# A two-layer transformer kernel whose planner takes its settings from a string: another string, read twice as often

## The chip, the cores and the metric

The kernel runs on one core of a Trainium2 chip. The metric is the device time of one execution in microseconds (us). A core has TensorE (PE, matmuls; PEld is its weight load), VectorE (DVE), ScalarE (ACT), GpSimd (POOL) and SyncE (SP, which issues the DMA transfers). Each engine works through its own list of instructions in order, and they wait for each other by semaphores.

## The reference

Two equal rounds of a 32-head attention block and a feed-forward block on 2048 tokens of width 512, with normalisation in front of each and residual additions. Input setup and casts are left out.

```python
def _A_ref(x, wqkv, wo):
    B, S, D = x.shape
    H = 32; Dh = D // H
    qkv = (lambda x, *d: x.transpose(*d))((x @ wqkv).reshape(B, S, 3, H, Dh), 2, 0, 3, 1, 4)
    q, k, v = qkv[0], qkv[1], qkv[2]
    scale = Dh ** -0.5
    scores = jnp.einsum("bhqd,bhkd->bhqk", q, k) * scale
    p = _softmax(scores, axis=-1)
    o = jnp.einsum("bhqk,bhkd->bhqd", p, v)
    return (lambda x, *d: x.transpose(*d))(o, 0, 2, 1, 3).reshape(B, S, D) @ wo

def _B_ref(x, w1, b1, w2, b2):
    y = _layernorm(x, axis=-1)
    h = _gelu(jnp.einsum("bsd,df->bsf", y, w1) + b1)
    return jnp.einsum("bsf,fd->bsd", h, w2) + b2

x = A_x
x = x + _A_ref(_layernorm(x, axis=-1), A_wqkv, A_wo)
x = x + _B_ref(_layernorm(x, axis=-1), B_w1, B_b1, B_w2, B_b2)
x = x + _A_ref(_layernorm(x, axis=-1), A_wqkv, A_wo)
x = x + _B_ref(_layernorm(x, axis=-1), B_w1, B_b1, B_w2, B_b2)
```

## The kernel before

**A program that plans itself.** The Python code does not write out its instructions in a fixed order. Every piece of work is a task for one engine, with the resources it reads and writes, a priority and an assumed duration. A scheduler (class `Sched`) simulates the five engines with these durations, always takes the task that can start first, and among the ready tasks of an engine the one of the smallest priority number. The result is one fixed list of instructions for each engine. What the chip runs is these lists, with semaphore waits between them; nothing is decided at run time.

**The work.** The two attention layers are called 1 and 3. The scores of a layer are cut into tiles of 128 keys by 512 queries (in layer 3's last units, 256 queries) for one head: 4096 tiles in all. Four heads make a head group; a segment is a head group's work for one unit of queries. For a tile:

- Line 1470, `score`: TensorE writes a score tile to one bank of PSUM, the accumulation memory. It uses one quarter of the array's rows, so up to four such matmuls run side by side.
- Line 1455: ScalarE takes the exponential of a group of tiles at once. Groups alternate between three banks and two, and a group is called an exponential group here. There are 1273 of them. In the opening part of layer 1, the first 64 groups, each has two.
- Lines 1555 and 1588: some tiles go to VectorE instead. Line 1555 approximates the exponential by shifting the score into the bits of a 16-bit float, and line 1588 makes three further shifted copies of two tiles at once, which are averaged by the value matmuls.
- Line 1658: value matmuls, which multiply the exponentials by the values and accumulate in bank 6. They use a quarter of the array's columns, so four run side by side. Line 1650 adds a correction row at the start of some segments.
- Line 1688 and after it: at the end of a segment VectorE transposes the accumulator, and the result is normalised.

Beside this run the linear parts: line 950 (queries, keys and values), 1737 (attention output), 1792 (first linear of the feed-forward block), 1835 (second linear). Line 1827 is the GELU on ScalarE, in which no exponential can run. Lines 927 and 1784 are transposing DMA transfers that bring normalised tokens in front of lines 950 and 1792.

**The bound over all keys.** Softmax needs an upper bound of each row's scores. It comes from the norms of all keys known so far: line 1157 takes the maximum, line 1159 transposes it on TensorE, line 1160 reduces, line 1162 takes a root on POOL, line 1163 builds a small matrix, line 1165 is a small matmul, line 1166 gives the scale, line 1196 makes the query tile. Layer 1 begins with the first 4 key blocks (part 0), layer 3 with the first 12. When all 16 are there, the bound is taken anew for part 1, and no score of part 1 can begin before.

**Fillers.** After planning, `refill` walks through TensorE's list and puts in matmuls on zeros (lines 1359, 1361, 1363; full array, row quarter, column quarter) where the plan has a gap on TensorE, as wide as the gap, as long as TensorE's planned use over the last 3.414 us is under 55%.

**The settings.** Class `Hint` holds six numbers that the planner reads, ten sets of them (`MODES`) and a string `ORDER`, in which a digit names a set. `flow_scores` counts the exponential groups with `gi` and reads the next digit after every `STEP` groups:

```python
if gi % Hint.STEP == 0:
    HINT.at(gi // Hint.STEP)
```

`D_IDLE` is how little work VectorE must have in front of it for a further tile to go there. `PV_LEAST` is how full a batch of value matmuls has to be. `HOLD_LATE` lengthens the time for which other matmuls are held back in front of scores that are due. `PV_NEAR` is how soon exponentials must be ready to be counted for a batch. `LIN2` caps the priority number of the later halves of linear work: 9 leaves it as it is, 0.9 puts these halves ahead of value matmuls, which have 1.0. `D_STEAL` lets VectorE take the last tile of a group of three where it has no work.

Of the kernel before, what the change touches and what calls it, by code (L numbers as in the profile page):

```python
# [507 lines left out]
class Hint:  # L508
    BASE = dict(D_IDLE=1.2, PV_LEAST=0.75, HOLD_LATE=0.4, PV_NEAR=0.7, LIN2=9, D_STEAL=0)
    MODES = (dict(), dict(D_IDLE=0.8), dict(D_IDLE=1.7), dict(PV_LEAST=0.6), dict(PV_LEAST=0.9), dict(HOLD_LATE=0.2), dict(HOLD_LATE=0.6), dict(PV_NEAR=0.4), dict(LIN2=0.9), dict(D_STEAL=1.0))  # L510
    STEP = 8
    ORDER = '0355550015621021500127723542380000551183094330404202738042440023535555121020004212005090903453421320027044075009578104471100282939255971103200420580357499912000'

    def mode(self, k):
        self.__dict__.update(self.BASE)
# [2 lines left out]
    def at(self, step):  # L518
        self.mode(int(self.ORDER[step], 36) if step < len(self.ORDER) else 0)

# [5 lines left out]
class Builder:  # L526
# [844 lines left out]
    def flow_scores(self):  # L1371
# [14 lines left out]
        while True:  # L1386
            if gi % Hint.STEP == 0:
                HINT.at(gi // Hint.STEP)
            self.advance()
# [629 lines left out]
```

## Time and profile before

| | |
|---|---|
| time, median of 3 runs | 1563.72 us (1562.58 to 1564.21) |
| span of the profiled execution | 1564.7 us |
| instructions | 39699 |
| ScalarE: exponentials, line 1455 | 1433.7 us busy, 1273 groups |
| VectorE: lines 1555 and 1588 | 638.1 and 559.9 us busy |
| TensorE: scores, line 1470 | 599.1 us busy |
| TensorE: value matmuls, line 1658 | 3525 on ScalarE's exponentials, 1083 and 3249 on VectorE's |
| TensorE: fillers | 487 of line 1359, 465 of line 1361, 1808 of line 1363 |
| granted TensorE clock, mean | 0.999 |

A group's row names the line, engine, operation and tiles, then the count, the busy time and the mean duration of one, and behind the second bar the idle time of the engine just before them and what ended it. Matmuls overlap, so their summed durations exceed the time they take. In rows in order of time, the first number is the start, the second the length, and a number in brackets the idle time before it with its releaser.

### The profile page before, as it was taken

How to read it: one execution, taken by the hardware profiler on the slowest of the kernel's cores; microseconds unless marked ns; L12 is line 12 of the kernel's file. 1: busy time of each engine (PE TensorE's matmuls, PEld its weight loads, DVE VectorE, ACT ScalarE, POOL GpSimd, SP SyncE). 2: the span in 40 equal slices, each digit the busy share in tenths (PEclk: the TensorE clock that was granted, in tenths of full speed). 3: DMA queues.
4: the chain of work that ended last, by engine and by line, in shares of the span. 5: the costliest groups of instructions: out<-in, count | busy, mean ns of one | idle time of the engine just before them, and what ended most of it. 6: DMA issues, size and time to landing. Idle time of an engine off the chain costs nothing.

```text
span 1564.7 us, 39699 instructions
## 1 busy us (share of the span) xinstructions
PE 1517.7 (97%) x16674; PEld 483.1 (31%) x16674; DVE 1459.9 (93%) x3256; ACT 1517.1 (97%) x1361; POOL 321.2 (21%) x558
## 2 busy tenths in 40 slices
PE   9999999999999999999999999999999999999998
PEld 3222222232223222222222322222232232344444
DVE  7699999999999899989999799999899999999894
ACT  8979999999999999999999999999999999999996
POOL 3575312001210021203222227410001000020100
PEclk9999999999999999999999999999999999999999
DMA  7663111203311232223832232310102000211110
GB/s 162 116 143 97 35 31 32 61 17 85 85 40 46 47 76 59 61 48 92 145 45 66 56 82 63 62 25 22 35 16 44 22 17 25 41 45 32 43 30 19
DMA packets 212451, 88.69 MB, mean 57 GB/s; under 512 B 183307, under 2 KB 207152, under 8 KB 212272
## 3 DMA queue, kind: packets, MB, share of 16 engines
q1 hardware_dynamic: 212272, 86.16, 24.9%
q8 instruction: 130, 2.13, 0.6%
q14 instruction: 49, 0.40, 0.1%
HBM read 34.65 MB, written 19.48 MB: 35 GB/s over the span
## 4 chain that ended last, share of the span: by engine, by line
ACT 34%; DVE 33%; PE 29%; issue 2%; POOL 1%; SPq 1%; DMA 1%; POOLq 0%; DVEq 0%
ACT PT L1455 33%; DVE dp L1555 13%; DVE dp L1588 10%; PE ps L1470 9%; PE ps L1658 8%; PE ps L1835 3%; PE ps L1792 2%; PE ps L950 2%; DVE accT L1688 2%; DVE n L1015 1%; ACT h L1827 1%; PE ps L1359 1%; DVE sq L991 1%; DVE h L1816 1%; PE ps L1068 1%
## 5 line engine op out<-in xcount | busy, mean ns | idle before, releaser
L1455 ACT ACTIVATE PT<-ps 128x1536 bf16<-128x1536 f32 (+1 forms) x1273 | 1433.7, 1285 | 28.5 <-PE ps L1470 25.1
L1555 DVE TENSOR_SCALAR dp<-ps 128x512 uint16<-128x512 f32 x960 | 638.1, 679 | 36.7 <-PE ps L1470 34.2
L1470 PE MATMUL ps<-QT,KT 32*128 32x512 bf16 (+1 forms) x4608 | 599.1, 359 | 19.6 <-ACT PT L1455 6.8
L1588 DVE TENSOR_SCALAR dp<-dp 128x1024 uint16<-128x1024 uint16 (+1 forms) x1452 | 559.9, 427 | 4.6 <-PE ps L1658 1.6
L1658 PE MATMUL ps<-PT,V 128*17 128x512 bf16 (+1 forms) x3525 | 483.8, 358 | 0.2 <-ACT PT L1455 0.2
L1658 PE MATMUL ps<-dp,vs 128*17 128x512 bf16 (+1 forms) x3249 | 467.6, 357 | 0.9 <-DVE dp L1588 0.4
L1470 PEld LDWEIGHTS ps<-QT,KT 32*128 32x128 bf16 x4608 | 161.1, 91 | 545.9 <-ACT PT L1455 286.3
L1196 POOL TENSOR_SCALAR QT<-qraw,scl,qbias 128x512 bf16<-128x512 bf16 (+1 forms) x83 | 72.3, 872 | 764.6 <-PE ps L1470 758.1
L1658 PE MATMUL ps<-dp,V 128*17 128x512 bf16 (+1 forms) x1083 | 227.1, 358 | 1.6 <-DVE accT L1688 0.6
L1363 PE MATMUL ps<-zw 128*32 128x448 bf16 (+23 forms) x1808 | 172.2, 321 | 0.8 <-DVE dp L1555 0.7
L1658 PEld LDWEIGHTS ps<-dp,vs 128*17 128x17 bf16 x3249 | 119.1, 88 | 115.4 <-issue 87.2
L1658 PEld LDWEIGHTS ps<-PT,V 128*17 128x17 bf16 x3525 | 116.9, 88 | 92.8 <-issue 78.5
L1361 PE MATMUL ps<-zw 32*128 32x444 bf16 (+5 forms) x465 | 132.8, 317 | 0.0
L1359 PE MATMUL ps<-zw 128*128 128x448 bf16 (+17 forms) x487 | 114.7, 334 | 3.2 <-DVE onec L754 2.1
L1792 PE MATMUL ps<-yT,wf 128*128 128x512 bf16 (+3 forms) x396 | 101.7, 361 | 3.1 <-DVE dp L1588 1.3
L950 PE MATMUL ps<-wqkv,xnT 128*128 128x512 bf16 x336 | 93.4, 382 | 5.8 <-DVE dp L963 2.2
L1363 PEld LDWEIGHTS ps<-zw 128*32 128x32 bf16 x1808 | 62.5, 95 | 27.8 <-DVE dp L1555 4.6
L1658 PEld LDWEIGHTS ps<-dp,V 128*17 128x17 bf16 x1083 | 55.5, 88 | 41.4 <-issue 24.1
L1221 POOL TENSOR_SCALAR vs<-V 128x340 bf16<-128x340 bf16 (+2 forms) x72 | 61.8, 859 | 26.1 <-PE ps L1658 15.1
L1688 DVE STREAM_TRANSPOSE accT<-ps 128x512 f32<-128x512 f32 (+1 forms) x88 | 57.8, 657 | 7.1 <-PE ps L1658 7.0
L1816 DVE TENSOR_SCALAR h<-ps,b1c 128x512 bf16<-128x512 f32 (+2 forms) x88 | 61.9, 703 | 1.9 <-PE ps L1792 1.5
L1359 PEld LDWEIGHTS ps<-zw 128*128 128x128 bf16 x487 | 37.6, 98 | 64.7 <-issue 40.0
(182 smaller groups left out, 885.5 us busy)
## 6 DMA issues: line engine op xcount, KB each, us to landing
vs<-vs_scr SPq DMA_DIRECT2D x56, 255.0 KB, 2.7
wf<-in_B_w_dram SPq DMA_DIRECT2D x90, 128.0 KB, 2.9
q_scr<-qk SPq DMA_DIRECT2D x20, 256.0 KB, 2.1
k_scr<-qk SPq DMA_DIRECT2D x12, 256.0 KB, 2.0
out_dram<-xres SPq DMA_DIRECT2D x16, 128.0 KB, 1.8
vs_scr<-vs SPq DMA_DIRECT2D x8, 255.0 KB, 2.9
xres<-in_A_x_dram SPq DMA_DIRECT2D x7, 256.0 KB, 3.2
v_scr<-vst SPq DMA_DIRECT2D x12, 136.0 KB, 1.7
```

The lines of the kernel that those rows point to most:

```text
L950: yield Task("pe", prio if c0 == 0 else min(prio, HINT.LIN2), [I(lambda e, c=c: e.matmul(self.ps[:, b, :], lhsT=xnT[:, c, :], rhs=self.wqk ...
L1359: fn = lambda e: e.matmul(self.ps[:, b, 0:w], lhsT=self.zw[:, 0:128], rhs=self.zw[:, 0:w], start=st, stop=st, skip_group_check=True)
L1361: fn = lambda e: e.matmul(self.ps[:, b, 0:w], lhsT=self.zw[32 * p:32 * p + 32, 0:128], rhs=self.zw[32 * p:32 * p + 32, 0:w], start=st, sto ...
L1363: fn = lambda e: e.matmul(self.ps[32 * p:32 * p + 32, b, 0:w], lhsT=self.zw[:, 0:32], rhs=self.zw[:, 0:w], start=st, stop=st, skip_group_c ...
L1455: S_.submit(Task("act", 1e-5 * gi, [I(lambda e, pt=pt, n=n, b0=b0: e.activation(out=self.PT[:, pt:pt + n, :], in_=self.ps[:, b0:b0 + n, :] ...
L1470: return [I(lambda e, kb=kb, i=i: e.matmul(self.ps[:, b, i * W:(i + 1) * W], lhsT=self.KT[32 * hp:32 * hp + 32, hg, kb * 128:(kb + 1) * 12 ...
L1555: self.S_.submit(Task("dve", 0.0, [I(lambda e: e.tensor_scalar(out=self.dp[:, u, w * 512:(w + 1) * 512], in0=self.ps[:, b, :], scalar1=BIT ...
L1588: yield Task("dve", pr, [I(lambda e, k=k, v=v: e.tensor_scalar(out=self.dp[:, v, 0:N], in0=self.dp[:, u, 0:N], scalar1=float(SHIFT[k]), sc ...
L1658: ops.append((nth[j, sh] + 0.1 * i, I(lambda e, hp=hp, v=v, ap=ap[:, i * W:(i + 1) * W], first=first and i == 0, W=W: e.matmul(self.ps[32 ...
L1688: yield Task("dve", 0.3, [I(lambda e: e.transpose(self.accT[:, a, 0:W], self.ps[:, ACCB, 0:W]), [("ps", ACCB)], [RA], 0.17 + 0.535 * W / 5 ...
L1792: yield Task("pe", pr if c0 == 0 else min(pr, HINT.LIN2), [I(lambda e, c=c: e.matmul(self.ps[0:M, b, off:off + W], lhsT=self.w1(fc, c), rh ...
L1816: S_.submit(Task("dve", pr - 0.7, [I(lambda e, fc=fc, M=M, b=b: e.tensor_scalar(out=hv[0:M, fc * W:(fc + 1) * W], in0=self.ps[0:M, b, 0:W] ...
```

## The change

The string is another one, of 319 digits instead of 160, and a digit holds for four exponential groups instead of eight. The sets of settings are the same. No other line differs (but for an empty line at the end of the file).

```diff
 class Hint:
     BASE = dict(D_IDLE=1.2, PV_LEAST=0.75, HOLD_LATE=0.4, PV_NEAR=0.7, LIN2=9, D_STEAL=0)
     MODES = (dict(), dict(D_IDLE=0.8), dict(D_IDLE=1.7), dict(PV_LEAST=0.6), dict(PV_LEAST=0.9), dict(HOLD_LATE=0.2), dict(HOLD_LATE=0.6), dict(PV_NEAR=0.4), dict(LIN2=0.9), dict(D_STEAL=1.0))
-    STEP = 8
-    ORDER = '0355550015621021500127723542380000551183094330404202738042440023535555121020004212005090903453421320027044075009578104471100282939255971103200420580357499912000'
+    STEP = 4
+    ORDER = '1000505400844554053031008034310130004043277211200001031009349005902383344374250110710071520000700010897013450230200545450055021090000330009921105703053220050405100500340302221091514024010003201130050000322000100000400300044000720830007030033701430000245354444034510580430030403022240093200204095050982000792049091440853'
```

The new string was found by following many partial orders of the work at once. How the two programs differ instruction by instruction is part of the working below.

## The prediction

> **What bounds the kernel now.** I read the page's busy shares first, then the groups by line, then the waits of ScalarE, then busy time by stage, then ScalarE and TensorE in order of time around the largest waits.
>
> ```profile
> PE 1517.7 (97%) x16674; PEld 483.1 (31%) x16674; DVE 1459.9 (93%) x3256; ACT 1517.1 (97%) x1361; POOL 321.2 (21%) x558
> ...
> L1455 ACT ACTIVATE PT<-ps 128x1536 bf16<-128x1536 f32 (+1 forms) x1273 | 1433.7, 1285 | 28.5 <-PE ps L1470 25.1
> ```
>
> PE's 97% holds zero matmuls (lines 1359, 1361, 1363) that only fill gaps, so it isn't the bound by itself. ACT has no filler: it idles 47.6 us of the span of 1564.7, and 25.1 of them stand before an exponential whose scores were not there. So the bound is the chain scores, exponential, with TensorE's order deciding how seldom ACT starves. ACT's busy time is a floor, its idle time is what an order can win. By stage (columns: window, length, then busy us of PE, PEld, DVE, ACT, POOL, clock, DMA share, GB/s):
>
> ```profile
> 0.00:80.00 80.00, 74.71 (x502) 24.27 (x503) 58.78 (x147) 73.29 (x86) 34.67 (x85) 1.00 0.68 139
> 80.00:140.00 60.00, 56.20 (x534) 16.74 (x533) 56.49 (x124) 50.95 (x48) 42.14 (x76) 1.00 0.62 136
> 140.00:800.00 660.00, 646.52 (x6594) 189.96 (x6590) 642.02 (x1409) 652.36 (x571) 123.06 (x201) 1.00 0.26 59
> 800.00:1000.00 200.00, 191.86 (x1973) 57.26 (x1965) 184.93 (x408) 194.51 (x176) 76.56 (x132) 1.00 0.30 66
> 1000.00:1540.00 540.00, 528.62 (x6934) 184.35 (x6926) 511.76 (x1159) 535.45 (x468) 43.29 (x60) 1.00 0.14 31
> 1540.00:1564.70 24.70, 19.82 (x159) 10.49 (x158) 5.88 (x13) 10.59 (x17) 1.48 (x4) 1.00 0.07 17
> ```
>
> ACT's idle by these stages is 6.7, 9.1, 7.6, 5.5, 4.5 and 14.1 us. The first 20 us and the last 24 hold fixed chains; some 26 us can be fought for. Three places hold half of that:
>
> ```profile
> 81.29 2.96 ACT L1455 ACTIVATE PT<-ps 128x1024 bf16<-128x1024 f32 x3 [0.21 <-PE ps L1470]
> 90.59 4.77 ACT L1455 ACTIVATE PT<-ps 128x1536 bf16<-128x1536 f32 x4 [6.35 <-PE ps L1470]
> ...
> 696.92 3.28 ACT L1455 ACTIVATE PT<-ps 128x1024 bf16<-128x1024 f32 x3 [2.43 <-PE ps L1470]
> ...
> 1215.70 1.45 ACT L1455 ACTIVATE PT<-ps 128x1536 bf16<-128x1536 f32 x1 [1.78 <-PE ps L1470]
> ```
>
> At 90.59 the next scores need the bound over all keys of layer 1 (lines 1157 to 1166). At 696.92 TensorE ran five matmuls of the second linear and 22 value matmuls between two scores. At 1215.70 it stood before line 1792, whose last transposed input was issued on SP at 1209.9 and let it begin at 1213.44 (the tile's landings take 2.5 to 4.2 us).
>
> **What the change does, step by step.** No line of code that issues work differs; other settings reorder it. So the cost lies in the order of the two programs' instructions, compared engine by engine. Counts: SP 524 and POOL 562 instructions in both, so no transfer is added. On ACT, 590 exponentials of three banks become 586 and 683 of two become 687. On DVE line 1555 goes from 960 to 964 tiles, and line 1588 gains 12 half-width rows (24 to 36). The fillers fall from 2760 to 2550.
>
> (a) ACT's work: by form a three-bank exponential takes 1515 ns and a two-bank one 1086, so 4 x 0.429 = -1.7 us. Between 0 (it comes back as waiting) and -1.7; I take -1.7, since ACT is the floor.
>
> (b) DVE's four tiles: 4 x 0.60 (two of line 1555 take 1.20 in the chain) plus 12 x 0.27 (the shortest of line 1588) = 5.6 us on an engine that idles 105 us. Cost 0, hidden by that idle time; up to +5.6 if all of it falls where DVE is full. Nearer to 0, since the tiles per eight heads differ by at most 4.
>
> (c) The first bound over keys. Rows before and after it:
>
> ```profile
> 82.79 0.39 PE L1470 MATMUL ps<-QT,KT 32*128 32x512 bf16 x2
> ...
> 87.02 0.23 PE L1159 MATMUL ps<-ident,nm 128*32 128x128 bf16 x1
> ...
> 89.94 0.82 PE L1470 MATMUL ps<-QT,KT 32*128 32x512 bf16 x7
> ```
>
> From 83.11, when line 950 follows the last score, to 89.94 are 6.83 us, of which 2.92 are the bound's own chain from line 1159 on. ACT's wait is that gap less the exponential still running (1.13, to 84.24) plus 0.65 from first score to exponential: 6.35. Before line 1159 the old program has six matmuls of line 950, eight of 1658 and fillers of 36 x 448 and 4 x 267 columns in four tiles side by side, 1.79 us. The new one has four of line 1650, eight of 1658 and 1341 columns (0.56 us). At 0.0606 us a value matmul (16 in 0.97 in the chain) that is 0.73 + 0.56 = 1.29, so the gap is 1.3 + 2.9 = 4.2, and the gain -2.6. Between 0 (the keys come no sooner) and -3.6 (the last two score groups now stand together, one exponential of 1.0 more to run meanwhile). I take -2.6, the rows' own difference.
>
> (d) A new bare stretch: at the second bound over keys of layer 3 the old program keeps scores between line 1159 and line 1165, the new one keeps none. Its 7 value matmuls (0.42) and 0.36 us of filler before line 1159, plus 2.92, make a gap of 3.7. Two exponentials (30 take 33.69 in the chain, so 2.25) can be queued: 3.7 - 2.25 + 0.65 = +2.1. Bounds 0 (a third is queued) and +3.2 (only 1.13 is).
>
> (e) The burst at 694 us is gone: outside the stretches behind a GELU, which hide under the 5 to 8 us that ACT spends on it, no score-free stretch over 1.5 us is left between the two bounds but (d). -2.4; 0 if another takes its place.
>
> (f) All other waits: 25.1 less 6.96 around 90.59, 2.43 and the 2.73 around 1215 leaves 13.0. Priced by rows (0.238 us a full matmul, five in 1.19 in the chain), score-free stretches exceed 1 us by 32.1 us in all in the old order and 26.1 in the new, 19% less: -2.5. Bounds 0 and -9.8: fillers on TensorE's own time fall from 147.3 to 135.8 us (columns at 0.417 ns; eight of 448 took 1.60), 1.7 of it in (c), and the rest would be all span.
>
> (g) Tail: 1344 columns of filler instead of 322 wait for the last head: +0.4 (0 to +0.9). The rest of the tail's order is the same.
>
> (h) Queues: transposes and loads on SP shift by a few places past each other. The nearest price is the stall at 1215: 1.78 + 0.56 + 0.39 = 2.73 us. I take 0, one such landing as before; -2.7 to +2.7 for none or two.
>
> Sum: -1.7 - 2.6 + 2.1 - 2.4 - 2.5 + 0.4 = -6.7. The profiled span of 1564.7 lies 1.0 over the median of 1563.72; 1558.0 of span is 1557.0 us.
>
> [...]
>
> ```profile
> 1212.00:1213.00 1.00, 0.10 (x2) 0.00 (x0) 1.00 (x4) 1.00 (x2) 0.00 (x0) 1.00 0.00 0
> ...
> 1214.00:1215.00 1.00, 1.00 (x7) 0.17 (x5) 0.00 (x0) 0.00 (x0) 0.00 (x0) 0.50 0.00 0
> ```
>
> The granted clock fell to 0.5 for 3.4 us after TensorE stood empty for only 1.34 us. [...]
>
> **The rivals.** Slower: late landings. TensorE is in order, so a matmul placed too early for its transposed input holds back the scores behind it, and the clock falls too. For it: 1215.70, and a new order sets all such places anew. Against it: the old order has one such stall in 1564 us. At 2.73 each, four more (6.7 + 3.1 over 2.73 is 3.6) decide: 1557.0 + 10.9 = 1567.9.
>
> No change: the waits move. If (d) costs the full 6.35 of the first bound (+4.2) and a burst like (e) stands elsewhere (+2.4), it ends at 1563.6. For it: (d) is plainly new. Against it: two groups can be queued there.
>
> More: all of the filler's fall is span, (f) at -9.8: 1549.7. For it: TensorE's real work is the same, so less filler means less gap. Against it: ACT has only 13 us of such waits.
>
> That the settings do nothing is out: the orders differ on all engines.
>
> **How the numbers follow.** This kernel's measurement can tell 0.2%, 3.1 us, from no change: faster is under 1560.6, slower over 1566.8. Forecast 0.50 and "more" 0.16: faster 0.66. The waits moved: same 0.20. Late landings, with DVE's 5.6 us falling in its full stages: slower 0.14. The forecast's own range is 1553 to 1560.5; with parts of both sides 1548 to 1567.
>
> **What would show it.** ACT's busy time near 1515.4; the wait at the first bound near 3.7 instead of 6.35; a new wait of about 2 before the first score after the second bound of layer 3; none over 2 in mid layer 1; DVE busier by 5 or 6. It's wrong if ACT's idle time doesn't fall below 45, or if the granted clock shows further drops.

## The result and the profile after

| | before | after |
|---|---|---|
| time, median | 1563.79 us (1562.58 to 1564.21, 4 runs) | 1553.3 us (1552.96 to 1553.99, 4 runs) |
| span of the profiled execution | 1564.7 us | 1551.2 us |
| ScalarE busy, and idle in that span | 1517.1 and 47.6 us | 1512.4 and 38.8 us |

The ratio is 0.9933, with a 95% interval of 0.9919 to 0.9947: 10.5 us faster, where 6.7 were forecast. The two profiled spans lie 13.5 us apart. Most of the 3 us between the two differences is explained by the first experiment.

The page of the kernel after, its busy shares and the groups of lines 1455, 1555 and 1588 (count, busy us, mean ns, idle time before and its releaser):

```profile
PE 1505.7 (97%) x16485; PEld 474.9 (31%) x16485; DVE 1465.6 (94%) x3272; ACT 1512.4 (97%) x1361; POOL 322.0 (21%) x558
...
L1455 ACT ACTIVATE PT<-ps 128x1536 bf16<-128x1536 f32 (+1 forms) x1273 | 1428.6, 1288 | 19.2 <-PE ps L1470 17.0
L1555 DVE TENSOR_SCALAR dp<-ps 128x512 uint16<-128x512 f32 x964 | 640.0, 678 | 27.2 <-PE ps L1470 25.5
...
L1588 DVE TENSOR_SCALAR dp<-dp 128x1024 uint16<-128x1024 uint16 (+1 forms) x1464 | 567.0, 427 | 3.6 <-PE ps L1658 0.9
```

Three things are to be read. ScalarE's waits for scores fell from 25.1 to 17.0 us. Its busy time fell by 4.7 us, although four tiles fewer explain only 1.7. VectorE is 5.7 us busier, at no cost that shows: its idle time behind line 1470 fell from 34.2 to 25.5 us.

ScalarE of the kernel after, in order of time, at the places that the prediction named (start, length, count, and in brackets the idle time before it):

```profile
87.40 9.15 ACT L1455 ACTIVATE PT<-ps 128x1536 bf16<-128x1536 f32 x8 [2.92 <-PE ps L1470]
97.35 3.71 ACT L1455 ACTIVATE PT<-ps 128x1536 bf16<-128x1536 f32 x3 [0.80 <-PE ps L1470]
...
692.76 8.25 ACT L1455 ACTIVATE PT<-ps 128x1536 bf16<-128x1536 f32 x7 [0.45 <-PE ps L1470]
...
933.36 11.60 ACT L1455 ACTIVATE PT<-ps 128x1536 bf16<-128x1536 f32 x10 [2.18 <-PE ps L1470]
```

The wait of 6.35 us at the first bound over all keys is 2.92 now. The wait of 2.43 behind the burst at 697 us is gone, and 0.45 is left near its place. The new wait of 2.18 stands before the first score after the second bound of layer 3, as foreseen. TensorE's rows around that bound show why (lines 1159 and 1165 are the bound's two matmuls):

```profile
928.17 0.79 PE L1470 MATMUL ps<-QT,KT 32*128 32x512 bf16 x5
...
929.97 0.23 PE L1159 MATMUL ps<-ident,nm 128*32 128x128 bf16 x1 [0.15 <-DVE nm L1157]
...
931.52 0.17 PE L1165 MATMUL ps<-krhs,sel 32*128 32x8 bf16 x1 [0.17 <-DVE krhs L1163]
...
932.92 0.81 PE L1470 MATMUL ps<-QT,KT 32*128 32x512 bf16 x6
```

From the end of one score row to the start of the next are 932.92 - 928.96 = 3.96 us without a score, against the 3.7 that the prediction worked out from counts of instructions.

**Waits that don't show in full as idle time.** The row of line 1455 gives a mean of 1288 ns, but consecutive exponentials overlap: from the start times of the trace, two-bank exponentials that follow each other without a wait start 904 ns apart and three-bank ones 1331, while one of them lasts 1086 and 1515 by its form. So a score that comes up to about 0.18 us late leaves no idle time and only makes the pitch longer, and one that comes later takes away these 0.18 us of overlap beside the idle time that shows. Summed over the pitches, start to start, of all exponentials in a row, and taking 904 and 1331 ns as free of waiting (first profiles; the list of waits names idle times over 0.15 us):

| us, from the start times | before | after |
|---|---|---|
| sum of the pitches | 1429.1 | 1416.0 |
| stretched beyond the free pitch, in all | 55.4 | 41.9 |
| where over 0.15 us of idle time shows (47 and 39 times) | 31.9 | 22.7 |
| where less idle time shows (51 and 27 times) | 11.8 | 6.0 |
| where none shows | 11.8 | 13.2 |

Of the 13.5 us less of stretching, 9.6 are idle time (28.3 and 18.7 us in these rows), and 3.9 are overlap that the kernel after doesn't lose. In the second profiles of both kernels (next section) it is 11.5 us, 7.9 of it idle. Stretches without any idle time are not fewer. What became fewer are the waits that show, 66 instead of 98, and each of them costs up to 0.18 us more than it shows.

### The profile page after: what moved, and what is told of

It reads as the page before. It is cut to its first block, busy times and chain, and to the rows that moved or that the text cites. A ratio compares the mean times of both kernels' runs of the same rounds, so it can differ in the third digit from the quotient of the medians.

```text
span 1551.2 us, 39363 instructions
## 1 busy us (share of the span) xinstructions
PE 1505.7 (97%) x16485; PEld 474.9 (31%) x16485; DVE 1465.6 (94%) x3272; ACT 1512.4 (97%) x1361; POOL 322.0 (21%) x558
## 4 chain that ended last, share of the span: by engine, by line
ACT 45%; DVE 29%; PE 22%; issue 2%; SPq 1%; DMA 1%; POOL 1%; POOLq 0%; DVEq 0%
ACT PT L1455 42%; DVE dp L1555 12%; DVE dp L1588 9%; PE ps L1470 7%; PE ps L1658 6%; PE ps L1835 2%; PE ps L950 2%; ACT h L1827 2%; PE ps L1359 2%; PE ps L1792 1%; DVE accT L1688 1%; DVE st L873 1%; DVE n L1015 1%; PE ps L1068 1%; PE ps L1363 1%
## 5 line engine op out<-in xcount | busy, mean ns | idle before, releaser
L1455 ACT ACTIVATE PT<-ps 128x1536 bf16<-128x1536 f32 (+1 forms) x1273 | 1428.6, 1288 | 19.2 <-PE ps L1470 17.0
L1555 DVE TENSOR_SCALAR dp<-ps 128x512 uint16<-128x512 f32 x964 | 640.0, 678 | 27.2 <-PE ps L1470 25.5
L1588 DVE TENSOR_SCALAR dp<-dp 128x1024 uint16<-128x1024 uint16 (+1 forms) x1464 | 567.0, 427 | 3.6 <-PE ps L1658 0.9
L1363 PE MATMUL ps<-zw 128*32 128x448 bf16 (+16 forms) x1679 | 163.6, 325 | 0.9 <-DVE dp L1555 0.7
L1361 PE MATMUL ps<-zw 32*128 32x444 bf16 (+4 forms) x443 | 131.7, 320 | 0.0
L1359 PE MATMUL ps<-zw 128*128 128x448 bf16 (+20 forms) x428 | 103.6, 340 | 4.4 <-DVE onec L754 2.1
L1363 PEld LDWEIGHTS ps<-zw 128*32 128x32 bf16 x1679 | 57.2, 95 | 25.8 <-DVE dp L1555 5.8
L1359 PEld LDWEIGHTS ps<-zw 128*128 128x128 bf16 x428 | 34.2, 99 | 61.5 <-issue 37.0
```

The costliest lines, as they stand in the source:

```text
L1359: fn = lambda e: e.matmul(self.ps[:, b, 0:w], lhsT=self.zw[:, 0:128], rhs=self.zw[:, 0:w], start=st, stop=st, skip_group_check=True)
L1361: fn = lambda e: e.matmul(self.ps[:, b, 0:w], lhsT=self.zw[32 * p:32 * p + 32, 0:128], rhs=self.zw[32 * p:32 * p + 32, 0:w], start=st, sto ...
L1363: fn = lambda e: e.matmul(self.ps[32 * p:32 * p + 32, b, 0:w], lhsT=self.zw[:, 0:32], rhs=self.zw[:, 0:w], start=st, stop=st, skip_group_c ...
L1455: S_.submit(Task("act", 1e-5 * gi, [I(lambda e, pt=pt, n=n, b0=b0: e.activation(out=self.PT[:, pt:pt + n, :], in_=self.ps[:, b0:b0 + n, :] ...
L1555: self.S_.submit(Task("dve", 0.0, [I(lambda e: e.tensor_scalar(out=self.dp[:, u, w * 512:(w + 1) * 512], in0=self.ps[:, b, :], scalar1=BIT ...
L1588: yield Task("dve", pr, [I(lambda e, k=k, v=v: e.tensor_scalar(out=self.dp[:, v, 0:N], in0=self.dp[:, u, 0:N], scalar1=float(SHIFT[k]), sc ...
```

## The experiments

**The two kernels once more, side by side.** No edit. They ask which of the differences belong to the programs and which to one execution.

> The kernel before, once more, for a second profile. Theory: the stall at 1215 us in its first profile (1.78 + 0.56 + 0.39 us of ScalarE's waiting, with the TensorE clock at 0.5 for 3.4 us) belonged to that one execution, a transfer that landed late; its span of 1564.7 stands 3 us above what the other executions leave for a span (1563.8 less the 2.1 that lie outside the span of the changed kernel). Then the new profile spans some 1561.7 us, shows no half clock in mid-kernel, and ScalarE waits for scores about 22.4 us in all instead of 25.1, with 6.35 at the first bound and 2.43 near 697 us as before. Rival: the stall belongs to the old order, which places a matmul too early for its input; then it is there again and the span is near 1564.7.

> The changed kernel, once more, as the reference of the two delays that run beside it. Theory: 1553.3 us again, ScalarE waiting 2.9 us at the first bound and 2.2 at the second bound of layer 3, since these waits stand in the order. Rival: they differ from execution to execution by a microsecond or more, and the gain can't be put down to places in the order.

The kernel before took 1564.03 us (against itself in the same session, 1563.44: ratio 1.0, interval 0.9991 to 1.0009), the kernel after 1552.42 us (ratio 0.9931, 0.9919 to 0.9944). ScalarE of the kernel before, second profile:

```profile
90.70 4.77 ACT L1455 ACTIVATE PT<-ps 128x1536 bf16<-128x1536 f32 x4 [6.35 <-PE ps L1470]
...
696.92 3.28 ACT L1455 ACTIVATE PT<-ps 128x1024 bf16<-128x1024 f32 x3 [2.43 <-PE ps L1470]
...
1216.92 9.14 ACT L1455 ACTIVATE PT<-ps 128x1536 bf16<-128x1536 f32 x8 [0.35 <-PE ps L1470]
```

The waits at 90.7 and 696.9 come back to the hundredth: they are of the program. The one at 1215.70, 1.78 us long with the clock at 0.50 for 3.4 us, did not come back: 0.35 is left, and the mean granted clock is 1.0, where the first profile has 0.999. That stall, 2.73 us in all, was of one execution of the two profiled. It accounts for most of the 3 us by which the first two profiles differ more than the medians do.

By how much the kernel after is ahead, exponential group for group, in these two profiles (difference of the start times):

| group of 1273 | 40 | 80 | 120 | 240 | 360 | 520 | 600 | 680 | 760 | 800 | 880 | 1000 | 1120 | 1240 | last |
|---|---|---|---|---|---|---|---|---|---|---|---|---|---|---|---|
| us ahead | -0.3 | 3.5 | 4.0 | 6.9 | 7.2 | 7.8 | 9.8 | 10.6 | 12.9 | 11.1 | 9.7 | 8.9 | 8.5 | 11.2 | 11.7 |

The lead is made at the first bound (3.5) and bit by bit from there to group 760 (another 9), 4 us are given back between groups 760 and 1120, and 3 made up again at the end; the tail adds 1.0, for a difference of spans of 12.7.

**A delay put in by hand, at four places.** Does a score that comes late cost as much wherever it is? To the kernel after, 14 matmuls on zeros of 448 columns are added in front of a score, 14 x 448 x 0.417 ns = 2.6 us of TensorE. The 0.417 is from the trace of the kernel after: line 1068's matmuls of 512 columns start 216 ns apart (median), those of 128 columns 56, and 160 / 384 = 0.417; zeros of 448 columns (line 1359) start 190 ns apart there. Nothing else is moved. The edit, with the place as the only difference:

```diff
-                fill(op)
+                fill(op), self.hold(op, put, banks)
...
+    def hold(self, op, put, banks):
+        if op.spec[6] and op.spec[6][0] == "row":
+            if self.rows == 128:
+                t0, b, st, due = banks(op, self.refilled.drain, 0.0)[0]
+                for _ in range(14):
+                    put(b, "full", 0, FILL_MOST, st)
+            self.rows += 1
```

Score 128 is the first one after the first bound over all keys:

> The changed kernel with 14 more zero matmuls of 448 columns in front of the first score after the first bound over keys; 14 x 0.187 = 2.6 us of TensorE at a place where ScalarE already waits. Theory (ScalarE's starvation is what an order wins or loses, and it is never made up): 2.6 us slower than the changed kernel, about 1555.9. Rival (slack further on takes it up, so that the shorter wait at this bound can't explain much of the gain): about 1553.3.

Score 790 is issued at 320 us, while ScalarE works on a GELU:

> The changed kernel with the same 14 zero matmuls, 2.6 us of TensorE, in front of a score of VectorE's at 320 us, while ScalarE is in the first GELU of layer 1 for 7.8 us. Theory (only ScalarE's starvation counts): less than 0.7 us slower than the changed kernel, 1553.3 to 1554.0. Rival (TensorE at 97% is a bound of its own, so any work added to it lengthens the kernel wherever it stands): 2.6 us slower, about 1555.9.

Score 2954 lies at 1120 us, in the middle of layer 3:

> The changed kernel with 14 zero matmuls of 448 columns (2.6 us of TensorE) in one block in front of a score at about 1120 us, where ScalarE runs 54 exponentials without a wait. The delays under the first bound and under a GELU cost 2.1 and 2.5 us, so TensorE is no free engine even there. Theory now (a delay counts as far as it outlasts the two exponential groups that are queued, and TensorE makes up the rest out of filler time): ScalarE waits 2.6 - 2.2 + up to 0.7 = 0.4 to 1.1 us, and the kernel takes 0.4 to 1.1 us more than the changed one. Rival (TensorE is a bound of its own): 2.6 us more.

And instead of one block, a single zero matmul in front of every 25th score from 1443 on (560 to 665 us), `self.rows in range(1443, 1793, 25)` with `range(1)`:

> The changed kernel with the same 14 zero matmuls one at a time, in front of every 25th score matmul between 560 and 665 us, each 0.19 us. Theory (short delays are hidden by the two queued groups, the same amount in one block isn't): less than 0.4 us more than the changed kernel. Rival (TensorE is a bound of its own): 2.6 us more, wherever and however it is spread.

| 2.6 us put in | time | ratio to before (interval) | new wait of ScalarE | behind the kernel after, at the last group |
|---|---|---|---|---|
| at the first bound | 1554.55 | 0.9942 (0.9930 to 0.9955) | 2.92 to 5.51 | 1.7 |
| under a GELU | 1554.95 | 0.9942 (0.9930 to 0.9955) | 2.25 behind the GELU | 1.5 |
| mid layer 3 | 1554.98 | 0.9937 (0.9925 to 0.9950) | 2.32 | 2.5 |
| 14 single ones | 1556.08 | 0.9943 (0.9929 to 0.9956) | none above 0.53 | 2.65 |

The second pair ran beside 1564.69 us of the kernel before, so the ratios are what compares. Against the 0.9931 of the kernel after they put the four at 1.7, 1.7, 0.9 and 1.9 us, give or take some 3 us, which can't tell a delay that comes through from one that doesn't. What follows rests on the traces. The last column is from the start times of one profile each, against the second profile of the kernel after (span 1550.5 us); against its first profile it is 0.8 us less. The step at the place of the delay is the same against both: 2.3, 2.5, 2.7 and 2.8 us.

At the first bound the wait takes the whole delay, as expected. Some 0.7 us are made up later, in one step at 370 us, where TensorE of the kernel after stands still for 1.15 us and TensorE of the delayed one for 0.22 (second profile of the kernel after, then the delayed kernel):

```profile
367.72 0.38 PE L950 MATMUL ps<-wqkv,xnT 128*128 128x512 bf16 x1 [1.15 <-DVE accT L1688]
```
```profile
369.15 0.38 PE L950 MATMUL ps<-wqkv,xnT 128*128 128x512 bf16 x1 [0.22 <-issue]
```

The other three did not go as expected. Under the GELU nearly nothing was expected to be lost, and ScalarE of that kernel shows this:

```profile
319.28 4.47 ACT L1827 ACTIVATE h<-h 128x5120 bf16<-128x5120 bf16 x1
...
325.72 2.37 ACT L1455 ACTIVATE PT<-ps 128x1536 bf16<-128x1536 f32 x2
330.34 18.33 ACT L1455 ACTIVATE PT<-ps 128x1536 bf16<-128x1536 f32 x16 [2.25 <-PE ps L1470]
```

The zeros ran during the GELU (TensorE, same kernel):

```profile
320.40 2.82 PE L1359 MATMUL ps<-zw 128*128 128x448 bf16 x14
323.16 0.39 PE L1470 MATMUL ps<-QT,KT 32*128 32x512 bf16 x1
...
329.70 0.60 PE L1470 MATMUL ps<-QT,KT 32*128 32x512 bf16 x4
```

and the kernel after at the same place:

```profile
320.33 0.39 PE L1470 MATMUL ps<-QT,KT 32*128 32x512 bf16 x1
...
326.99 0.60 PE L1470 MATMUL ps<-QT,KT 32*128 32x512 bf16 x4
```

From score 790 to the next row of four scores are 6.66 us in the kernel after and 6.54 in the other: TensorE makes up 0.12 of the 2.8 us. It is not waiting for ScalarE there. It works off a fixed list of scores, value matmuls, matmuls of the second linear and zeros nearly without a gap, so what is late at the start of this stretch is late at its end. Two exponential groups stand ready behind the GELU, and they last 2.37 us; the delay comes through after them.

Mid layer 3 the block gives a bare wait of 2.32, and 2.49 of it are left at the end. Split into 14 pieces of 0.19 us it gives no such wait, and yet 2.65 at the end. ScalarE of that kernel in the stretch with the 14 pieces, and then the second profile of the kernel after there:

```profile
641.46 9.20 ACT L1455 ACTIVATE PT<-ps 128x1536 bf16<-128x1536 f32 x8 [0.47 <-PE ps L1470]
650.90 2.36 ACT L1455 ACTIVATE PT<-ps 128x1536 bf16<-128x1536 f32 x2 [0.25 <-PE ps L1470]
653.49 6.89 ACT L1455 ACTIVATE PT<-ps 128x1536 bf16<-128x1536 f32 x6 [0.22 <-PE ps L1470]
660.68 8.62 ACT L1455 ACTIVATE PT<-ps 128x1536 bf16<-128x1536 f32 x8 [0.30 <-PE ps L1470]
669.74 2.37 ACT L1455 ACTIVATE PT<-ps 128x1536 bf16<-128x1536 f32 x2 [0.45 <-PE ps L1470]
```
```profile
611.09 58.33 ACT L1455 ACTIVATE PT<-ps 128x1536 bf16<-128x1536 f32 x52 [0.23 <-PE ps L1470]
669.70 2.37 ACT L1455 ACTIVATE PT<-ps 128x1536 bf16<-128x1536 f32 x2 [0.28 <-PE ps L1470]
```

Both rows of x2 start at 669.7, but the delayed kernel is two groups behind: 94 exponentials since 560.9 against 96 (70 and 44 in the rows left out). The same 94 exponentials take 108.84 us in the delayed kernel and 106.37 (560.69 to 667.06) in the kernel after, 2.47 us more. Of these 1.66 are idle time (2.25 against 0.59 us, with the idle times too short for a bracket), and 0.8 are in pitches alone. So the expectation that two queued groups cover a short delay was wrong at these places. A reading that fits all four: TensorE's list, zeros included, has hardly a gap there, so it stays late, and a delay is made up only where TensorE stands still, as at 367 us. Whether the gaps would take up a delay if no zeros stood in them was not tested.

**Fillers.** 2550 of the kernel's matmuls are zeros. Do they hold up scores? First, let the plan leave 0.10 us more free at the end of each gap, so that 2039 are left, with all other work in the same order:

```diff
-FILL_SLACK = 0.02
+FILL_SLACK = 0.12
```

> The changed kernel whose fillers end 0.12 us before the planned start of the next real matmul instead of 0.02; 2039 fillers instead of 2550, the order of all other work as it is. The four delays showed that 0.19 us in front of a score passes through whole, so a filler that ends late holds up ScalarE too. Theory (some of ScalarE's short waits, about 14 us of stretched pitch between exponentials, come from fillers that reach into the start of a score): 1 to 5 us faster than the changed kernel, 1548 to 1552. Rival 1 (fillers yield in time): 1553. Rival 2 (the clock lives on them): the granted clock falls in more places than the end, and the kernel is slower than the changed one by 2 us or more.

1555.73 us, ratio 0.9942 (0.9929 to 0.9956), not faster. The sum of the pitches is 1418.6 us, against 1415.3 for the kernel after in its second profile. One stretch of its profile, by windows of time (length, busy us of PE, PEld, DVE, ACT and POOL, granted clock, DMA share, GB/s):

```profile
757.00:758.00 1.00, 0.03 (x1) 0.00 (x0) 0.55 (x3) 1.00 (x2) 0.70 (x2) 1.00 1.08 175
758.00:759.00 1.00, 0.75 (x6) 0.34 (x6) 1.00 (x4) 0.62 (x2) 0.00 (x0) 1.00 1.22 271
...
761.00:764.00 3.00, 3.00 (x29) 0.68 (x29) 2.24 (x7) 2.16 (x3) 0.00 (x0) 0.50 0.94 197
764.00:769.00 5.00, 5.00 (x46) 1.57 (x39) 3.92 (x10) 4.58 (x4) 0.77 (x1) 0.50 1.17 190
```

TensorE stood empty for about 1 us at 757, the clock fell to one half at 760 and stayed there for 10.24 us, and the kernel's lag behind the kernel after (second profile) grew from 0.6 to 4.0 us over it; 3.25 are left at the last group. Up to the drop it was not ahead either, and exponentials with idle time before them are not fewer (68 against 66). So the theory failed: the columns of zeros fell by 38%, and no wait of ScalarE went with them.

Then without any filler:

```diff
-                fill(op)
+                pass
...
-                if op.spec[6] and not any(
+                if op.spec[6] and False and not any(
```

> The changed kernel without any filler, the order of all other work as it is. No gap of TensorE in mid-kernel is longer than 2.2 us of filler was, at the bounds over keys. Theory (the granted clock falls after a short stretch of low use, as after 1.34 us of emptiness in the first profile of the kernel before): many stretches at half clock, and slower than the changed kernel by 20 us or more. [...]

1596.43 us, ratio 1.0196 (1.0177 to 1.0215), as the theory had it. The mean granted clock is 0.947, and it is 0.93 to 0.97 in the six stages that the prediction lists, where the kernel after has 1.00 in all six. The stage from 140 to 800 us of that kernel, and its waits for scores (total, times, longest):

```profile
140.00:800.00 660.00, 598.50 (x5251) 154.91 (x5301) 626.76 (x1377) 636.02 (x558) 117.96 (x194) 0.94 0.25 58
```
```profile
ACT PT L1455 <- PE ps L1470: 49.1, 78, 2.9
```

Where the kernel after has ScalarE busy for 654.27 us of these 660, this one has 636.02, at a mean clock of 0.94. By the ratios (1.0196 - 0.9933, of 1564) the fillers are worth 41 us.

**The string itself.** What does a string carry? With the empty string the first set of settings holds throughout:

```diff
-    ORDER = '1000505400844554053031008034310130004043277211200001031009349005902383344374250110710071520000700010897013450230200545450055021090000330009921105703053220050405100500340302221091514024010003201130050000322000100000400300044000720830007030033701430000245354444034510580430030403022240093200204095050982000792049091440853'
+    ORDER = ''
```

> The same planner with an empty string, so that the first set of settings holds throughout. The order has 20.4 us more of filler on TensorE's time than the old one (168.5 against 147.3 less the different mix; 938 tiles on VectorE instead of 960). Theory (a string is worth what it saves in TensorE's gaps, at about 0.9 us of time for 1 us of filler, as between the two kernels): about 1583 us. Rival (a string is only fine tuning on an order that is good anyway): within 5 us of the kernel before, 1564 to 1569.

1609.6 us, ratio 1.0285 (1.0271 to 1.0300): both expectations were well short. By the ratios the old string is worth some 45 us over no choice at all, the new one 55. Its page:

```profile
PE 1560.4 (97%) x16799; PEld 490.8 (31%) x16799; DVE 1451.0 (90%) x3207; ACT 1535.3 (96%) x1367; POOL 317.2 (20%) x558
```

VectorE takes 938 tiles there instead of 960, so ScalarE has 22 more (22 x 0.43 = 9.5 us); and ScalarE's waits for scores are 40.9 us instead of 25.1.

And the new opening put in front of the old rest: the first 18 digits of the new string (72 groups, past the first bound), then the old string from group 72 on, each digit twice. STEP is 4, and every group after 72 has the setting that it has in the kernel before:

```diff
-    STEP = 8
-    ORDER = old
+    STEP = 4
+    ORDER = new[:18] + ''.join(d + d for d in old)[18:]
```

> The new string for the first 72 exponential groups, which reach past the first bound over keys, and the old string from there on. Theory 1 (the gains have places, and each stays where it was won): the opening's 3.6 us and nothing else, about 1560. Theory 2 (a digit is good only behind the digits before it, since the planner's state at the splice differs and all later choices with it): the old string's rest is worth no more than arbitrary settings, and the kernel takes 1575 us or more, though the wait at the first bound is the new, short one of about 3 us.

1604.86 us, ratio 1.0255 (1.0241 to 1.0269). ScalarE of this kernel at the first bound, and its waits for scores:

```profile
87.30 9.14 ACT L1455 ACTIVATE PT<-ps 128x1536 bf16<-128x1536 f32 x8 [2.93 <-PE ps L1470]
```
```profile
ACT PT L1455 <- PE ps L1470: 46.9, 99, 4.1
```

The gain at the bound is kept, 2.93 instead of 6.35, and at group 120 the kernel is 2.3 us ahead of the kernel before. Then it falls behind, 6 us by group 480, 17 by 600, 28 by 960, 42 by 1200, and ends within 5 us of the empty string. Behind this other beginning the old digits are worth hardly anything. What a digit does depends on where every engine of the plan stands when it is read, so this string was no list of good settings for places of the kernel, but one path. It is the only splice that was tried.

## Why the prediction held, point by point

The likeliest case was right, faster by many small waits removed, and its range of 1553 to 1560.5 held the time, by only 0.3 us: the second session's 1552.42 lies just below it. Its own forecast of 1557.0 was 3.7 us too slow. By its terms, in the profiles:

| term | forecast | measured |
|---|---|---|
| (a) four tiles fewer on ScalarE | -1.7 | -1.7 by count, not measured apart |
| (b) VectorE's 5.6 us more | 0 | 5.7 more busy, no cost seen |
| (c) first bound over all keys | -2.6 | -3.4 |
| (d) second bound of layer 3 | +2.1 | +2.2 |
| (e) burst at 694 us | -2.4 | -2.4 |
| (f) all other waits | -2.5 | -1.9 in idle time, -3.0 in busy time beyond (a) |
| (g) tail | +0.4 | -0.3 |
| (h) late landings | 0 | -2.7 in the first two profiles, none in the medians |

The measured terms without (h) come to -10.5, as the change of the medians does. They are read from the first two profiles, so this says only that nothing large is left out.

- **(c)** was right in its place and its bounds of 0 to -3.6, and 0.8 too small as taken. The stretch without a score is as worked out: 4.26 us, from 82.71, when line 1650 follows the last score, to 86.97, against 4.2. What was mis-sized is what ScalarE has left to do in it, 1.78 us (82.55 + 1.94 = 84.49) instead of 1.13, and the time from score to exponential, 0.43 (87.40 - 86.97) instead of 0.65. The prediction had seen that the last two score groups now stand together, and gave it the weight of a bound only.
- **(d)** came out at 2.18. Two groups were queued there, as taken; the row of x2 before it lasted 2.36.
- **(e)** is right in its result. That no other stretch without scores over 1.5 us is left is not so: the kernel after has them at 164, 366 and 799 us, 1.67 to 1.96 us long, but the longest wait behind one is 0.68. Its premise, that a stretch behind a GELU is hidden, holds for the stretches of the plan: the longest, 7.1 us from 1445.2 to 1452.3, has no wait behind it (row below, from the kernel after). The delay under the first GELU shows that this doesn't make added work there free: 1.5 of its 2.6 us are left at the end.

```profile
1450.80 50.15 ACT L1455 ACTIVATE PT<-ps 128x1536 bf16<-128x1536 f32 x46
```

- **(f)** is the mis-sized step: "Priced by rows [...] score-free stretches exceed 1 us by 32.1 us in all in the old order and 26.1 in the new, 19% less: -2.5". That counts waits as ScalarE's idle time. The idle part was priced well enough (-2.5 against -1.9). What was put at nothing is the overlap of 0.18 us that a wait takes away beside the idle time that shows: there are 66 such waits instead of 98. By the start times the overlap that is lost fell by 3.9 us in all (5.3 at these waits, less 1.4 more in stretches without idle time), by the busy shares 3.0. The prediction's own sign, ScalarE busy "near 1515.4", came out at 1512.4.
- **(g)**: the wait before line 1889 fell from 7.09 to 6.80 us, though 1022 columns more of zeros stand there. So they cost nothing that shows.
- **(h)**: the price was that of a stall which the second profile doesn't have. The rival built on it, four more such landings, did not come about: the mean granted clock is 1.00 in all stages of the kernel after.

Of the other rivals, the waits did move as "no change" had it, to (d), but (d) cost 2.2 and not 6.35. "More", in which all of the fall in filler time is span, would have given 1549.7. The fall was 11.5 us and the time fell by 10.5, so it fits these two kernels nearly as well as the forecast does. As a law it fails: the kernel with wider slack has 511 fillers fewer and was not ahead even before its clock fell, and the empty string's is 21 us longer in filler time (168.5) and 46 longer in time.

**What stays open.** Whether the gain is from the finer grain of four groups or from the wider search was not told apart: a string of the new kind read every eight groups would have another history from the first digit on. Nor is it shown which single digit gives which part.

## What to carry to other kernels

Where instructions overlap on the engine that bounds, sum start-to-start times, not idle times: 3.9 of the 13.5 us gained here, and a third of what 14 delays of 0.19 us cost, are in no idle time. Take a second profile of the same kernel before a stall is given a price: the one at 1215 us was of one execution, while those at 90 and 697 us repeated to the hundredth. Settings that were found as a sequence can belong to the whole program they were found with: here, behind another beginning, the old ones were worth at most 5 of their 45 us, so after a change upstream look whether they still hold.

## Not expected of the hardware

How long TensorE stood empty did not by itself tell where the granted clock would fall. One drop in the kernel without fillers, by windows of 1 us (columns as above):

```profile
453.00:454.00 1.00, 0.29 (x4) 0.10 (x3) 1.00 (x4) 1.00 (x2) 0.00 (x0) 1.00 0.00 0
454.00:455.00 1.00, 1.00 (x14) 0.21 (x11) 1.00 (x4) 1.00 (x2) 0.00 (x0) 1.00 0.00 0
455.00:456.00 1.00, 0.11 (x3) 0.00 (x0) 1.00 (x3) 1.00 (x2) 0.84 (x2) 0.71 0.00 0
456.00:457.00 1.00, 0.93 (x9) 0.22 (x11) 1.00 (x4) 1.00 (x3) 1.00 (x1) 0.50 0.00 0
...
468.00:469.00 1.00, 1.00 (x13) 0.15 (x10) 1.00 (x3) 1.00 (x2) 0.00 (x0) 0.50 0.82 235
469.00:470.00 1.00, 0.84 (x9) 0.35 (x6) 1.00 (x5) 1.00 (x2) 0.00 (x0) 0.96 0.07 27
```

TensorE was empty for 0.71 us of the window at 453 and for 0.89 us of the one at 455, in which the clock fell; it was 0.50 from 456 to 469. In the same profile emptiness of this size was also followed by full clock:

```profile
412.00:413.00 1.00, 0.17 (x3) 0.00 (x0) 1.00 (x3) 1.00 (x2) 0.00 (x0) 1.00 0.81 300
413.00:414.00 1.00, 0.88 (x10) 0.20 (x10) 1.00 (x2) 1.00 (x3) 0.00 (x0) 1.00 0.29 101
414.00:415.00 1.00, 0.43 (x5) 0.09 (x2) 1.00 (x4) 1.00 (x1) 0.00 (x0) 1.00 0.00 0
415.00:416.00 1.00, 0.61 (x11) 0.21 (x11) 1.00 (x5) 1.00 (x2) 0.46 (x1) 1.00 0.00 0
```

These four windows hold 0.83 + 0.12 + 0.57 + 0.39 = 1.91 us of emptiness, the two from 126 to 128 us hold 0.61 + 0.85 = 1.46, and the one at 428 us holds 0.95. The clock is 1.00 in them and in all windows of the next 5 us behind each. In the first profile of the kernel before, 1.34 us of emptiness had 3.4 us at half clock behind them. What decides was not found out here.
